# Rows of gate scores spread over the partitions by products in all four batches, in a kernel with an order written out by hand

## The chip, the core and the metric

One core of a Trainium2 chip runs the program. The metric is the device time of one execution in microseconds (us); the median of several runs is compared. Five instruction queues run beside each other: PE (matrix products; its weight loads are shown as PEld), DVE (vector), ACT (scalar), POOL, and SP, which only issues transfers. Each works through its own instructions strictly in order, and waits where an operand or a buffer is not ready. Transfers run on 16 DMA engines.

## What is computed

Four batches of a local attention with block summaries, and behind it a layer in which only the 128 best-scored tokens of a batch go through a two-layer network:

```
scores_l = scale * q @ k.T            # kept where |i - j| < 16
scores_s = scale * q @ max-of-32-keys # plus log(32)
x        = softmax([scores_l, scores_s]) @ [v, mean-of-32-values]
...
scores = einsum('bsd,d->bs', x, w_gate)           # 4 x 768
top    = the 128 largest scores of a batch
out    = x
out[top] = x[top] + sigmoid(scores[top]) * (relu(x[top] @ w1) @ w2)
```

There are 4 batches, 8 heads of 64, 768 tokens, 512 columns, and 1024 hidden columns.

## The kernel before

The heads are taken in pairs (16 pairs, n = 0 to 15, four of each batch), and each pair in three groups of 256 tokens, so that there are 48 steps. The steps of the first three batches go pair by pair; in batch 3 they go group by group over its four pairs. A step i is a chain of short operations: S (scores of two steps at once, PE), M (mask and minimum, DVE), E (exponent, on ACT; on POOL or DVE it is only the subtraction and the exponent comes with the next copy), T (transposes, PE), V (copy out of PSUM, ACT), A (products with the values, PE), R and N (divide, DVE or ACT). Ahead of a pair stand its loads k, q, vt or v, and kmax, vsum, spr, ms, vx, vk, mt, mk, md, which make the block summaries and put the values in place.

Behind the last step of a batch b:

- st{b}.g stores 256 rows of x into the output, ga{b}.u (or gq and gl in batch 3) makes the gate scores of 128 tokens, one column of a 128 x 6 tile `sss` for each u (DVE).
- The 768 scores must then stand as one row in every partition (tile `rows`, 128 x 768). In batches 0 to 2 this is rt (one transpose on PE of the 128 x 6 tile, L412), rk (copy to SBUF on ACT, L415), rw (write of 3 KB to DRAM, L418) and rr (read back, 3 KB into each of the 128 partitions, L421). In batch 3 it is ro and ri: ro{b}.g transposes two score columns, each broadcast to 128 columns (two products on PE, L426), and ri{b}.g copies the 256 columns out of PSUM (ACT or DVE, L430), three times over.
- cmp{b}.u (six of them, L439 and L441, DVE) compares, rank (21 small products), rb, rs, oh, pick and pk make the indices of the 128 tokens, gat (POOL, L504) gathers their rows from the output in DRAM into the tile xe, with fx, fxh, fxl (transpose and split into two parts), f1 (first layer, two halves of three products each), fr, ft, fh, fl (relu, transposes, split), f2 (second layer), fo (scale and add) and sca (POOL, L638), which scatters the rows.
- The weights come in eight loads w0 to w7 through three staging tiles that the network uses again later (h, hh, hl). wh and wl (16 each) split them into a high and a low part, wl always on POOL. So fh0.0, which writes hh, must follow wl13, and fl0.0, which writes hl, must follow wl15.

All order is set by one long text, ORDER, a list of 900 names: `T0@3` is an operation and the PSUM bank it uses, `E4:s` an operation and its engine (v is DVE, s ACT, g POOL). The list is walked once and each name issues its instructions, so each engine's queue is the list's own order, that of SP too. Nothing else moves anything.

Of the kernel before, what the change touches and what calls it, by code (L numbers as in the profile page):

```python
# [54 lines left out]
k0 ones:g zero:v clrv1:g onep0:g q0 onep2:v clrv0:v cst warm@4 kmax0:v spr0:s S0@56 M1.0:v M0.0:v M0.1:v E0:s T0@3 vt0  # L55
M1.1:v vsum0:v casts:v k1 E1:s vt1 onep1:g T1@2 ms0:g vx0.0@5 q1 vk0.0:s vx0.1@1 kmax1:v vk0.1:s spr1:g vx0.2@4 V0:s
vsum1:v V1:v S2@71 vk0.2:s k2 q2 S4@30 k3 M2.1:v M2.0:v M3.1:v A1@5 R1:v ms1:g M3.0:v vt2 N1:s A0@1 E2:g M5.1:v
vx1.2@2 T2@7 R0:v vt3 M4.0:v M4.1:v V2:s vx1.1@4 vk1.1:s vx1.0@5 A2@7 E4:s M5.0:v kmax2:v q3 T4@3 E3:g k4 k5 vt4 w2 q5
q4 vk1.2:s E5:g kmax3:v vk1.0:s R2:v spr2:g T5@6 V4:s S6@02 vsum2:v N0:v vsum3:v M6.1:v M7.0:v spr3:s ms2:s T3@1
M6.0:v V5:s A4@4 R4:v M7.1:v V3:s A5@6 E7:s clrv3:g clrv2:g A3@5 E6:g S8@01 ms3:g N4:v gate R5:v R3:v N2:v vx2.0@4 k6  # L60
N3:s T6@3 vx3.1@2 vsum4:g V6:s M9.0:v N5:v M8.0:v M8.1:v kmax4:v T7@5 vx3.2@3 M9.1:v vk3.1:s vk3.2:v vx3.0@7 vk2.0:s
kmax5:v A6@6 V7:s spr4:s S10@40 E8:s T8@5 w0 V8:s vt6 vx2.2@1 vk3.0:s M10.0:v M11.0:v vx2.1@2 M10.1:v M11.1:v vk2.1:s
vk2.2:s R6:v E10:s E9:g N6:v S12@45 T9@0 M12.0:v A7@3 A8@7 spr5:g wh4:g wl4:g kmax6:v M12.1:v R7:v M13.0:v R8:v E11:g
N7:v V9:s S14@62 E12:s M15.0:v ms4:g wh0:g A9@1 vx4.2@0 M14.1:v T10@3 N8:s R9:v vk4.2:s T12@7 M15.1:v N9:v V10:s
vsum6:g wh5:g M13.1:v vx4.0@0 T11@1 V12:s V11:s q7 ga0.1:v ga0.0:v M14.0:v vt5 vsum5:v ms6:g A10@7 A11@4 R11:v E13:s
vk4.0:s R10:v E14:g spr6:s ms5:s k7 q6 S16@52 N11:v N10:v M16.1:v M17.1:v wl0:g kmax7:v st0.0 vx5.0@4 E15:s ga0.5:v w1
vx4.1@1 k8 T13@6 vk4.1:s T14@2 S18@17 vx5.1@3 M16.0:v V14:s ga0.2:v vk5.0:s A12@2 T15@4 M17.0:v E16:s vk5.1:s vx5.2@0
V15:s vx6.0@3 ga0.3:v M18.1:v V13:s vk6.0:s R12:v E17:g M19.0:v M18.0:v spr7:g wh2:g wh3:g wh1:s wl1:g wl2:g N12:v
vk5.2:s ga0.4:v vx6.2@4 M19.1:v E18:v vx6.1@5 A15@6 vk6.2:s R15:v rt0@0 st0.1 vt7 q8 vsum7:v vk6.1:s rk0:s S20@23
M20.0:v k9 A13@4 M20.1:v R13:v T16@5 N15:s T17@1 A14@0 V16:s A16@6 M21.1:v M21.0:v vt8 ms7:s vx7.0@2 N13:s V17:s  # L70
kmax8:v k10 R14:v R16:v kmax9:v N14:s T18@3 wl3:g V18:s vk7.0:s S22@41 vsum8:v E19:g T19@0 M22.0:v E20:g M22.1:v rw0
M23.1:v T20@7 A18@2 M23.0:v wl5:g E21:g R18:v N16:v spr9:g ms8:s sx0:s spr8:s S24@35 V19:s E23:s vt9 N18:v kmax10:v w4
rr0 A19@4 A17@0 R19:v M24.1:v E22:g M25.1:v R17:v wh8:s vsum9:g k11 q9 T22@2 V22:s vx7.1@1 N19:v N17:v M25.0:v vx8.2@5
vx8.0@4 T21@2 w5 wh9:s q10 vx7.2@0 vk8.2:s vk7.1:s V21:s M24.0:v vx8.1@6 vk8.1:s ms9:s vk7.2:s V20:s cmp0.2:v T23@5
cmp0.5:v vk8.0:v S26@12 sg0:v cmp0.0:v vt10 st0.2 A21@6 wl8:g E24:g sh0:g cmp0.1:v E25:s M27.1:v R21:v M26.1:v M27.0:v
M26.0:v A20@4 vt11 R20:v wh10:s spr10:s T24@3 A22@0 w3 wl9:g N21:s V24:s S28@27 E26:g kmax11:v N20:s V23:s E27:g
vx9.0@1 T25@3 ga1.1:v cmp0.4:v cmp0.3:v M28.0:v vk9.0:s wh11:s vx9.1@4 A23@5 R23:v R22:v A24@6 vk9.1:s V25:s T26@4
rb0:v N23:s V26:s rank0@1 R24:v N22:v vsum11:v S30@35 rs0:v M28.1:v vsum10:g w6 ms10:s vx10.1@4 T27@1 M29.0:v E28:s
wh6:s V27:s M31.0:v M30.0:v T28@0 vk10.1:s M29.1:v vx10.2@2 ga1.2:v vx10.0@7 wl11:g wl10:g N24:v vk10.2:s vk10.0:s
ms11:g st1.0 q11 k13 spr11:s vx9.2@3 vk9.2:s vx11.0@1 vk11.0:s ga1.4:v vx11.2@7 vk11.2:s A25@4 k12 oh0:v ga1.0:v V28:s  # L80
wh12:g pick0@6 fg0:v M31.1:v pk0:v w7 A27@3 S32@21 q12 R27:v vt13 A26@0 ga1.5:v E29:s M30.1:v ga1.3:v gat0:g kmax12:v
N27:s E30:g A28@7 R28:v rt1@3 vx11.1@5 E31:s N28:v rk1:s M33.0:v R26:v T30@6 T29@3 T31@7 vk11.1:s wl6:g V30:s S34@65
V31:s k14 rw1 M32.0:v fx0@2 M32.1:v V29:s E32:s kmax13:v A29@7 M33.1:v R25:v N25:v A30@3 st1.1 M35.0:v M34.1:v fxh0:s
wh13:g T32@4 V32:s N26:s vsum13:v M34.0:v M35.1:v kmax14:v f10.0@1 wh15:g f10.1 A31@0 sx1:s sg1:v R29:v fxl0:v vt12
rr1 vsum12:v q13 E33:s vt14 v12.0 A32@4 E35:s R31:v N31:v R32:v spr12:g wl12:g wl15:g wh7:g f10.3@6 wl7:g cmp1.0:v
vt15 st1.2 f10.2 N29:s T33@2 k15 q14 mt12@5 fr0.0:s wh14:g f10.4 V33:s N32:s R30:v E34:g wl13:g wl14:g f10.5 N30:v
cmp1.2:v vsum14:g mt13@1 T34@0 cmp1.5:v mk12:s md12.1 v13.0 ft0.0@4 T35@2 fr0.1:s spr13:s V34:s fh0.0:s V35:s ft0.1@5
md12.0 cmp1.3:v vsum15:g sh1:g cmp1.1:v S36@76 fl0.0:v M37.0:v A35@2 A34@0 A33@3 cmp1.4:v M37.1:v mk13:s M36.1:v R35:v
fh0.1:s E37:s rb1:v N35:s f20.0@1 M36.0:v rank1@4 f20.1 rs1:v R33:v N33:s oh1:v ga2.0:v md13.1 E36:s kmax15:v R34:v
N34:s spr15:g T37@4 f20.2 pick1@2 mt14@6 mk14:s spr14:s f20.3 f20.4 T36@0 fl0.1:v pk1:v ga2.5:v V37:s V36:s ga2.3:v  # L90
fg1:v ga2.2:v q15 S38@73 v12.1 M38.1:v S40@05 ga2.1:v mt15@6 md13.0 mk15:s md14.0 gat1:g M39.1:v v13.1 f20.5 ga2.4:v
fo0.0:v fx1@2 fxh1:s A36@4 v15.1 M38.0:v sx2:s fxl1:v M40.0:v R36:v M39.0:v rt2@6 M40.1:v sca0:g rk2:s f11.3@1 E38:g
E39:v f11.4 S42@37 N36:s M41.1:v A37@4 M41.0:v R37:v T38@6 E41:g M42.0:v v15.0 E40:s M43.1:v M42.1:v f11.5 T39@2 E42:g
T40@7 N37:s V39:s S44@40 M43.0:v sg2:v E43:g S46@23 M44.1:v M45.1:v v14.0 md14.1 M44.0:v rw2 M45.0:v V38:s v14.1 V40:s
T41@5 A38@0 E44:g sh2:g V41:s A40@7 M46.1:v M47.0:v M47.1:v T43@4 rr2 md15.0 T44@6 A41@5 md15.1 A39@3 R38:v N38:v
M46.0:v cmp2.0:v V43:s T42@4 E45:g st2.0 R40:v N40:v cmp2.5:v R39:v E47:s st2.1 cmp2.1:v cmp2.3:v E46:s f11.0@2 R41:v
N41:v fr1.1:s V42:s gq3.1:v cmp2.4:v gq3.0:v T46@0 f11.1 f11.2 A43@4 N39:s R43:v A42@3 R42:v V44:s fr1.0:s cmp2.2:v
ft1.0@6 fh1.0:s ft1.1@1 T47@5 T45@7 N43:s V46:s N42:v rb2:v rank2@3 A44@2 fl1.0:v gl3.0:v V45:s A46@0 V47:s gl3.1:v
A45@6 A47@5 rs2:v fh1.1:s oh2:v R46:v R47:v pick2@4 st2.2 fg2:v pk2:v fl1.1:v R45:v ro3.0@7 gq3.2:v R44:v ri3.0:v
N47:s N46:s N45:s gq3.3:v f21.0@3 f21.1 f21.2 gat2:g f21.3 N44:s gl3.2:v cmp3.1:v gl3.3:v gq3.4:v cmp3.0:v ro3.1@1  # L100
fx2@6 f21.4 f21.5 fxh2:s gq3.5:v ri3.1:v gl3.4:v cmp3.2:v gl3.5:v f12.3@2 ro3.2@4 f12.0@5 f12.1 cmp3.3:v ri3.2:s sx3:s
fxl2:v f12.2 fo1.0:v f12.4 sca1:g cmp3.4:v cmp3.5:v rank3@7 rb3:v sg3:v f12.5 sh3:g st3.2 st3.0 fr2.0:s ft2.0@5 rs3:v
oh3:v pick3@1 fg3:v pk3:v fr2.1:s ft2.1@0 fh2.0:s fh2.1:s fl2.0:v f22.0@7 f22.1 f22.2 f22.3 st3.1 gat3:g fl2.1:v fx3@6
f22.4 f22.5 fxh3:v f13.0@5 fo2.0:v sca2:g f13.1 fxl3:v f13.2 f13.3@7 f13.4 f13.5 fr3.0:v ft3.0@4 fr3.1:v ft3.1@0
fh3.1:v fh3.0:s fl3.0:v f23.0@3 f23.1 f23.3@6 f23.4 f23.5 f23.2 f23.6 fl3.1:v f23.9 f23.7 f23.8 fo3.0:v f23.10 f23.11
fo3.1:v sca3:g
# [4 lines left out]
def attn_moe(ctx: ExitStack, tc: tile.TileContext, q, k, v, vt, vs, w1, w2, cst, line, out, cap):  # L111
# [50 lines left out]
    srow = [const.tile([NU, 128], F32, name=f"srow{i}") for i in range(1)]  # L162
# [20 lines left out]
    def put(name, engs, fn, *a):  # L183
        ops[name] = (engs, fn, a)
# [224 lines left out]

    def rows_turn(e, b):  # L410
        rps[b] = ps = bank("m")
        nc.tensor.transpose(out=ps[0:NU, 0:128], in_=s_(b), identity=ident)  # L412

    def rows_keep(e, b):
        copiers[e](out=srow[0], in_=rps[b][0:NU, 0:128])  # L415

    def rows_write(e, b):
        nc.sync.dma_start(out=line[b].rearrange("(u t) -> u t", u=NU), in_=srow[0])  # L418

    def rows_read(e, b):  # L420
        nc.sync.dma_start(out=rank_tiles(b)[0], in_=line[b].unsqueeze(0).broadcast_to([128, S]))  # L421

# [317 lines left out]
    for b in range(B):  # L740
        for g in range(NG):
# [10 lines left out]
            if b == B - 1:  # L752
                put(f"ro{b}.{g}", "t", rows_of, b, g)
                put(f"ri{b}.{g}", "sv", rows_into, b, g)
        if b < B - 1:
            put(f"rt{b}", "t", rows_turn, b)
            put(f"rk{b}", "sv", rows_keep, b)
            put(f"rw{b}", "d", rows_write, b)
            put(f"rr{b}", "d", rows_read, b)
# [106 lines left out]
```

## Time and profile before

| | us |
|---|---|
| median of 3 runs | 171.59 (171.19 to 171.59) |
| the profiled execution | 172.67 |
| its span, first to last instruction | 170.4 |
| busy in the span: PE / DVE / ACT / POOL | 157.7 / 137.7 / 107.8 / 88.2 |
| granted TensorE clock | 1.00 |

Busy time of an engine is the time in which at least one of its instructions runs; matrix products are pipelined, so the step from one group's start to the next group's start (its pitch) is often shorter than the duration of one. Views speak of the span, whose zero is the first instruction. The profiled execution lies 2.3 us above its span and 1.1 us above the median.

### The profile page before, as it was taken

How to read it: one execution, taken by the hardware profiler on the slowest of the kernel's cores; microseconds unless marked ns; L12 is line 12 of the kernel's file. 1: busy time of each engine (PE TensorE's matmuls, PEld its weight loads, DVE VectorE, ACT ScalarE, POOL GpSimd, SP SyncE). 2: the span in 40 equal slices, each digit the busy share in tenths (PEclk: the TensorE clock that was granted, in tenths of full speed). 3: DMA queues.
4: the chain of work that ended last, by engine and by line, in shares of the span. 5: the costliest groups of instructions: out<-in, count | busy, mean ns of one | idle time of the engine just before them, and what ended most of it. 6: DMA issues, size and time to landing. Idle time of an engine off the chain costs nothing.

```text
span 170.4 us, 6154 instructions
## 1 busy us (share of the span) xinstructions
PE 157.7 (93%) x2273; PEld 128.9 (76%) x2273; DVE 137.7 (81%) x718; ACT 107.8 (63%) x319; POOL 88.2 (52%) x134
## 2 busy tenths in 40 slices
PE   7979999998999979899899999699999999999980
PEld 2448788887878968788787978478889787788870
DVE  4297999999999989999999799686899997533620
ACT  0365888998989799899978785264778721300100
POOL 7013787985499968965999823406510204202002
PEclk9999999999999999999999999999999999999999
DMA  5999999989998999999888995978600292101001
GB/s 204 349 414 419 410 381 367 319 310 314 347 335 321 260 368 383 369 361 348 298 311 258 317 205 94 270 202 278 222 1 4 63 349 86 50 12 62 4 0 62
DMA packets 14897, 41.44 MB, mean 243 GB/s; under 512 B 1538, under 2 KB 2708, under 8 KB 14868
## 3 DMA queue, kind: packets, MB, share of 16 engines
q1 hardware_dynamic: 14228, 38.95, 66.1%
q0 software_dynamic: 640, 2.10, 3.8%
q8 instruction: 18, 0.29, 0.7%
q14 instruction: 11, 0.09, 0.1%
HBM read 33.10 MB, written 7.35 MB: 237 GB/s over the span
## 4 chain that ended last, share of the span: by engine, by line
PE 38%; DVE 20%; issue 14%; DMA 12%; POOL 7%; ACT 5%; POOLq 1%; SPq 0%; DVEq 0%
PE z_A_a L354 8%; PE z_T_t L337 7%; PE z_S_sa L305 6%; DVE sm L317 4%; PE z_warm_m L673 4%; DVE lt L439 4%; DMA rows<-line 4%; PE z_f10p_f L571 3%; DMA xe<-out_dram,idx 3%; DMA line<-srow 3%; DVE lt L441 3%; ACT p L328 2%; DMA hl<-in_w_dram 2%; POOL p L331 2%; PE z_S_sb L305 2%
## 5 line engine op out<-in xcount | busy, mean ns | idle before, releaser
L328 ACT ACTIVATE p<-sm,mxs 128x120 f32<-128x120 f32 x92 | 29.1, 399 | 5.0 <-DVE mxs L317 4.9
L331 POOL TENSOR_TENSOR p<-sm,mxs 128x480 f32<-128x480 f32 x23 | 23.5, 1026 | 15.6 <-PE z_T_t L337 6.1
L337 PE MATMUL z_T_t<-cs,p 128*120 128x128 f32 x192 | 29.5, 280 | 1.5 <-ACT p L328 1.2
L354 PE MATMUL z_A_a<-v,pt 121*64 121x65 f32 x768 | 29.1, 225 | 0.1
L354 PEld LDWEIGHTS z_A_a<-v,pt 121*64 121x64 f32 x768 | 24.9, 137 | 5.2 <-issue 1.8
L305 PE MATMUL z_S_sa<-slots,qb 64*64 64x120 f32 x384 | 25.6, 269 | 0.9 <-DMA qb<-in_q_dram 0.9
L337 PEld LDWEIGHTS z_T_t<-cs,p 128*120 128x120 f32 x192 | 21.5, 137 | 6.0 <-ACT p L328 2.8
L305 PE MATMUL z_S_sb<-slots,qb 64*64 64x120 f32 x384 | 24.9, 268 | 1.2 <-issue 0.6
L317 DVE CUSTOM_DVE_ANT_0 sm<-z_S_sa,cs 128x120 f32<-128x120 f32 x96 | 22.3, 275 | 4.4 <-PE z_S_sb L305 3.5
L370 ACT ACTIVATE x<-z_A_a,rdens 128x64 f32<-128x64 f32 x96 | 22.0, 329 | 5.1 <-DVE rdens L359 5.0
L317 DVE CUSTOM_DVE_ANT_0 sm<-z_S_sb,cs 128x120 f32<-128x120 f32 x96 | 22.3, 275 | 2.8 <-PE z_S_sb L305 2.6
L305 PEld LDWEIGHTS z_S_sa<-slots,qb 64*64 64x64 f32 x384 | 19.9, 132 | 5.1 <-issue 2.9
L305 PEld LDWEIGHTS z_S_sb<-slots,qb 64*64 64x64 f32 x384 | 19.6, 132 | 0.9 <-ACT x L370 0.8
L638 POOL DMA_INDIRECT out_dram<-h,idx x4 | 4.0, 996 | 28.7 <-DVE h L632 28.7
L344 ACT ACTIVATE pt<-z_T_t 120x512 f32<-120x512 f32 x25 | 15.2, 611 | 5.8 <-PE z_T_t L337 3.8
L229 DVE TENSOR_REDUCE kss<-slots 128x24 f32<-128x768 f32 x16 | 15.0, 943 | 1.3 <-DMA slots<-in_k_dram 1.3
L317 DVE DVE_READ_ACCUMULATOR2_ANT mxs<- 128x1 f32 x192 | 15.8, 82 | 0.0
L342 ACT COPY pt<-z_T_t 120x512 f32<-120x512 f32 x22 | 12.9, 600 | 3.3 <-PE z_T_t L337 3.0
L399 DVE SCALAR_TENSOR_TENSOR junkv<-x,cs 128x512 bf16<-128x512 f32 x18 | 13.0, 724 | 0.1
L439 DVE TENSOR_SCALAR_CACHE_REDUCE lt<-rows,sss 128x256 bf16<-128x256 f32 (+4 forms) x20 | 12.0, 601 | 0.5 <-DMA rows<-line 0.5
L504 POOL DMA_INDIRECT xe<-out_dram,idx x4 | 4.7, 1184 | 14.5 <-DVE idx L499 11.5
L373 DVE TENSOR_TENSOR x<-z_A_a,rdens 128x256 f32<-128x256 f32 x24 | 9.7, 414 | 0.3
(195 smaller groups left out, 329.8 us busy)
## 6 DMA issues: line engine op xcount, KB each, us to landing
slots<-in_k_dram SPq DMA_DIRECT2D x16, 552.0 KB
slots<-in_vs_dram SPq DMA_DIRECT2D x12, 552.0 KB
qb<-in_q_dram SPq DMA_DIRECT2D x16, 384.0 KB
out_dram<-x SPq DMA_DIRECT2D x12, 512.0 KB
v<-in_v_dram SPq DMA_DIRECT2D x8, 292.5 KB
hl<-in_w_dram SPq DMA_DIRECT2D x3, 512.0 KB
hh<-in_w_dram SPq DMA_DIRECT2D x3, 512.0 KB
slots<-in_vt_dram SPq DMA_DIRECT2D x4, 384.0 KB
```

The source lines that it names most:

```text
L229: nc.vector.tensor_reduce(out=ks.rearrange("p (u m) -> p u m", u=NU), in_=kv, axis=AX.X, op=ALU.max)
L305: nc.tensor.matmul(out=sc[k][h][par * QT:(par + 1) * QT, uu * NC:(uu + 1) * NC], lhsT=qt[rows, t * QT:(t + 1) * QT], rhs=kt[rows, window(t ...
L317: nc.vector.tensor_tensor_reduce(out=sm[:, j, :], in0=sc[i][h][:, uu * NC:(uu + 1) * NC], in1=cs[:, c0:c0 + NC], scale=-1.0 / D ** 0.5, sc ...
L328: nc.scalar.activation(out=pb[i % 3][:, j, :], in_=sm[:, j, :], func=AF.Exp, scale=-1.0, bias=mx[:, j:j + 1])
L331: engines[e].tensor_tensor(out=pb[i % 3], in0=sm, in1=mx.unsqueeze(2).broadcast_to([128, 4, NC]), op=ALU.subtract)
L337: nc.tensor.transpose(out=ps[0:NC, j * 128:(j + 1) * 128], in_=pb[i % 3][:, j, :], identity=ident)
L342: copiers[e](out=dst, in_=src)
L344: nc.scalar.activation(out=dst, in_=src, func=AF.Exp, scale=-1.0)
L354: nc.tensor.matmul(out=av[par * QT:(par + 1) * QT, j, :], lhsT=pt[0:NC + 1, j, par * QT:(par + 1) * QT], rhs=vw[n % NVB][0:NC + 1, par, u, ...
L370: nc.scalar.activation(out=x_(b, g)[:, j // 2, c:c + D], in_=av[:, j, 0:D], func=AF.Copy, scale=rden[:, j:j + 1])
L399: nc.vector.scalar_tensor_tensor(out=junkv, in0=x_(b, u // 2)[:, u % 2, :], scalar=1.0, in1=gate, op0=ALU.mult, op1=ALU.mult, accum_out=s_ ...
L439: nc.vector.tensor_scalar(out=lt[u][:, 0:c], in0=rows[:, 0:c], scalar1=s, scalar2=0.0, op0=ALU.is_lt, op1=ALU.add, accum_out=accs[:, b % 2 ...
```

## The change

The rows are made by ro and ri in all four batches. rt, rk, rw and rr go, with the tile `srow` and the DRAM lines. And the list is a new one from its first name to its last: it holds 906 names instead of 900, and nearly every operation stands at another place; some are on another engine (exponents: 23 on POOL, 23 on ACT, 2 on DVE before; 26, 21, 1 now. vsum: 6 on POOL before, 5 now. N: 24 on ACT before, 22 now. wh: 10 on POOL before, 8 now). Of the new ri, eleven are on ACT and one on DVE.

```
 ORDER = """
-k0 ones:g zero:v clrv1:g onep0:g q0 onep2:v clrv0:v cst warm@4 kmax0:v spr0:s S0@56 M1.0:v M0.0:v M0.1:v E0:s T0@3 vt0
...
-fxl2:v f12.2 fo1.0:v f12.4 sca1:g cmp3.4:v cmp3.5:v rank3@7 rb3:v sg3:v f12.5 sh3:g st3.2 st3.0 fr2.0:s ft2.0@5 rs3:v
...
+k0 onep1:v clrv2:v cst vt0 zero:v warm@1 casts:v kmax0:v clrv3:g q0 onep2:v spr0:g k1 onep0:g S0@17 q1 clrv0:g vsum0:v
...
+ri3.2:s cmp3.5:v cmp3.2:v cmp3.4:v f12.4 sg3:v rank3@4 rb3:v rs3:v sca1:g fr2.0:s st3.1 ft2.0@0 f12.5 sh3:g fh2.0:s
...
-    def rows_turn(e, b):
-        rps[b] = ps = bank("m")
-        nc.tensor.transpose(out=ps[0:NU, 0:128], in_=s_(b), identity=ident)
-
-    def rows_keep(e, b):
-        copiers[e](out=srow[0], in_=rps[b][0:NU, 0:128])
-
-    def rows_write(e, b):
-        nc.sync.dma_start(out=line[b].rearrange("(u t) -> u t", u=NU), in_=srow[0])
-
-    def rows_read(e, b):
-        nc.sync.dma_start(out=rank_tiles(b)[0], in_=line[b].unsqueeze(0).broadcast_to([128, S]))
...
-            if b == B - 1:
-                put(f"ro{b}.{g}", "t", rows_of, b, g)
-                put(f"ri{b}.{g}", "sv", rows_into, b, g)
-        if b < B - 1:
-            put(f"rt{b}", "t", rows_turn, b)
-            put(f"rk{b}", "sv", rows_keep, b)
-            put(f"rw{b}", "d", rows_write, b)
-            put(f"rr{b}", "d", rows_read, b)
+            put(f"ro{b}.{g}", "t", rows_of, b, g)
+            put(f"ri{b}.{g}", "sv", rows_into, b, g)
```

Three places of the new order. First, the start of DVE's queue, up to its first work on keys (zero feeds the 16 warming products on PE; pt and v are buffers that are cleared). Before:

```order
L667 MEMSET zero 128x1
L664 MEMSET pt_78 32x512
L654 MEMSET v_72 32x24x64
L655 MEMSET v_72 32x24
L656 MEMSET v_72 120x24
L229 TENSOR_REDUCE kss<-slots 128x24
```

And now:

```order
L650 MEMSET pt_77 32x512
L640 MEMSET v_74 32x24x64
L641 MEMSET v_74 32x24
L642 MEMSET v_74 120x24
L653 MEMSET zero 128x1
L669 CAST iotab<-cs 128x128
L670 TENSOR_SCALAR tri<-cs 128x128
L671 CAST tok<-cs 128x24x2
L228 TENSOR_REDUCE kss<-slots 128x24
```

The memset of zero now stands behind one pt and one v buffer, and the three casts that need the constants stand ahead of the first kmax.

Second, SP's queue around the write and the read back of batch 0 (slots are the loads of keys and values, qb those of queries, hh and hl weights on their way). Before:

```order
L418 DMA line<-srow_105 6x128
L217 DMA slots<-in_vs_dram 128x1104
L517 DMA hh<-in_w_dram 128x1024
L421 DMA rows<-line 128x768
L206 DMA slots<-in_k_dram 128x1104
L210 DMA qb_68<-in_q_dram 128x768
L517 DMA hl<-in_w_dram 128x1024
L210 DMA qb_69<-in_q_dram 128x768
```

And now:

```order
L378 DMA out_dram<-x_87 128x2x512
L503 DMA hh<-in_w_dram 128x1024
L216 DMA slots<-in_vs_dram 128x1104
L503 DMA hl<-in_w_dram 128x1024
L205 DMA slots<-in_k_dram 128x1104 x2
L209 DMA qb_69<-in_q_dram 128x768
```

The two transfers of the score row are gone; the load into qb_69 still follows the weights of hl.

Third, PE's queue from the last product of rank1 to the first of pick1 (oh is what pick multiplies). Before:

```order
L450 MATMUL z_rank_m<-one,lt_115 128x1
L624 MATMUL z_f20p_y<-w2l,hh 128x512 x4
L337 MATMUL z_T_t<-cs,p_93 120x128 x4
L624 MATMUL z_f20p_y<-w2h,hl 128x512 x4
L493 LDWEIGHTS oh
```

And now:

```order
L436 MATMUL z_rank_m<-one,lt_114 128x1
L577 MATMUL z_ft0p_f<-cs,h 128x128 x4
L610 MATMUL z_f20p_y<-w2h,hh 128x512 x4
L610 MATMUL z_f20p_y<-w2l,hh 128x512 x4
L610 MATMUL z_f20p_y<-w2h,hl 128x512 x4
L610 MATMUL z_f20p_y<-w2h,hh 128x512 x4
L479 LDWEIGHTS oh
```

Between rank1 and pick1 stood two groups of f2 and one T; now there are four groups of f2 and one half's ft.

## Rows read from the trace of the kernel before

**Rows 1.** The page, part 1: busy us, share, instructions of each engine.

```profile
PE 157.7 (93%) x2273; PEld 128.9 (76%) x2273; DVE 137.7 (81%) x718; ACT 107.8 (63%) x319; POOL 88.2 (52%) x134
```

**Rows 2.** Busy time by window: start:end, length, each engine, clock, DMA share, GB/s.

```profile
21.00:99.00 78.00, 74.72 (x1356) 63.95 (x1355) 74.67 (x410) 69.16 (x203) 64.54 (x93) 1.00 0.95 330
81.00:91.00 10.00, 9.40 (x131) 7.79 (x132) 9.76 (x50) 8.61 (x29) 9.92 (x12) 1.00 0.86 289
110.00:165.00 55.00, 54.45 (x588) 45.92 (x588) 38.54 (x197) 22.62 (x69) 11.62 (x18) 1.00 0.32 107
```

**Rows 3.** Timeline of PE: start, duration, line, [idle before <- releaser]: turn and ro.

```profile
48.21 0.27 PE L412 MATMUL z_rt_m<-cs,sss 128*6 128x128 f32 x1 [0.27 <-ACT v L284]
48.42 0.31 PE L305 MATMUL z_S_sa<-slots,qb 64*64 64x120 f32 x1
...
139.63 0.38 PE L426 MATMUL z_ro3p_m<-cs,sss 128*128 128x128 f32 x2
139.77 1.18 PE L571 MATMUL z_f12p_f<-w1h,xh 128*128 128x512 f32 x4
```

**Rows 4.** Lines L426, L415 and L430: count, duration ns min/median/max, first and last start.

```profile
L426 PE MATMUL z_ro3p_m<-cs,sss x6: 271/272/302, 132.1 to 139.7; 128*128 128x128 f32 x6
L415 ACT COPY srow<-z_rt_m x3: 238/248/255, 49.0 to 110.9; 6x128 f32<-6x128 f32 x3
L430 ACT COPY rows<-z_ro3p_m x1: 374/374/374, 140.0 to 140.0; 128x256 f32<-128x256 f32 x1
```

**Rows 5.** Chain that ended last, in time: start, us, what; then one row of waits.

```profile
54.35 6.24 DMA rows<-line
```

```profile
DVE lt L439 <- DMA rows<-line: 0.5, 1, 0.5
```

**Rows 6.** Timeline of SP, then of PE: a query load and the scores behind it.

```profile
58.16 0.66 SPq L210 DMA_DIRECT2D qb<-in_q_dram  x1
```

```profile
62.97 0.31 PE L305 MATMUL z_S_sa<-slots,qb 64*64 64x120 f32 x1 [0.86 <-DMA qb<-in_q_dram]
```

**Rows 7.** Timeline of PE: rank1, pick1, and the transposes behind the gather of batch 1.

```profile
99.19 0.68 PE L450 MATMUL z_rank_m<-one,lt 128*128 128x1 bf16 x21
102.11 0.30 PE L493 MATMUL z_pick_m<-tok,oh 128*128 128x5 bf16 x6
```

```profile
109.38 0.63 PE L544 MATMUL z_fx_m<-cs,xe 128*128 128x128 f32 x4 [1.60 <-DMA xe<-out_dram,idx]
```

**Rows 8.** Timeline of all engines at the start, down to the scores S6.

```profile
0.92 6.53 PE L673 MATMUL z_warm_m<-zero 128*128 128x512 bf16 x16 [0.92 <-DVE zero L667]
1.02 0.48 DVE L664 MEMSET pt<- 32x512 f32 x1 [0.16 <-issue]
...
1.78 1.34 DVE L654 MEMSET v<- 32x1536 f32 x1 [0.27 <-issue]
...
9.66 2.45 PE L337 MATMUL z_T_t<-cs,p 128*120 128x128 f32 x8 [1.23 <-ACT p L328]
...
20.97 0.31 PE L305 MATMUL z_S_sa<-slots,qb 64*64 64x120 f32 x1
```

**Rows 9.** Timeline of all engines near the end.

```profile
140.81 1.00 POOL L638 DMA_INDIRECT out_dram<-h,idx  x1 [6.91 <-DVE h L632]
...
144.05 0.60 ACT L580 ACTIVATE h<-z_f12p_f 128x512 f32<-128x512 f32 x1 [3.52 <-DMA out_dram<-h,idx]
```

```profile
158.18 0.60 PE L591 MATMUL z_ft3p_f<-cs,h 128*128 128x128 f32 x4
159.13 0.66 PE L591 MATMUL z_ft3p_f<-cs,h 128*128 128x128 f32 x4 [0.35 <-DVE h L582]
159.54 0.72 PE L624 MATMUL z_f23p_y<-w2h,hh 128*128 128x256 f32 x4
```

**Rows 10.** A row of waits, then a group of instructions: busy us, mean ns, idle before.

```profile
DVE hl L536 <- POOL vss L246: 1.1, 1, 1.1
```

```profile
L529 POOL TENSOR_TENSOR w2l<-hl,w2h 128x512 fp32r<-128x512 f32 x4 | 5.1, 1293 | 0.0
```

## What the change was predicted to do

> **What bounds the kernel now.** I read the busy times first, then the windows, then the waits and the chain, and last the timeline at the few places where PE stops. PE is busy for 157.7 of 170.4 us [rows 1], and the windows show how: from 110 to 165 us it is busy 54.45 of 55 us [rows 2], so in that last third the end is simply the sum of PE's work, whatever the other engines do. From 21 to 99 us PE and DVE are both busy 74.7 of 78 us and ACT 69.2 [rows 2]; there three engines hand short pieces to each other, and a loss on any of them is soon one of PE. The clock is granted in full in every window. The time is therefore PE's work plus the few places where PE stops. What the change takes away, in batch 0 a read back of 6.24 us behind its write, stands on the chain that ended last, but the only wait for it in the whole trace is 0.5 us of DVE [rows 5]: the transport itself was covered. So the removal pays where it held up other things, and the products have to be paid on the busiest engine.
>
> **The products.** Batches 0 to 2 get nine ro of two products each and lose three rt. By pitch, a pair of products moved PE's next start by 0.14 us and the rt by 0.21, which was late itself by 0.27 us [rows 3]; I take 0.20 for a pair, a little over its row, since in the middle more of them will come between unlike work, and 0.15 for an rt: 9 x 0.20 - 3 x 0.15 = **+1.35 us**. Bounds: by full duration, 272 ns for each product [rows 4], it would be 18 x 0.272 - 3 x 0.273 = +4.1 us; nothing at all if every pair falls into a stop of PE. I choose the pitch because in the middle PE has a next instruction ready nearly always.
>
> The Trainium skill, "TensorE: Matmul & The Clock Gate", Part 4: PE-mode transpose, gives about 275 ns for a 128 x 128 transpose inside a kernel, most of it access latency. The 272 ns rows agree with the figure, but the pitch says that the latency overlaps with the next instruction; by the page's figure as a cost the products would be an estimated +4.1 us instead of +1.35.
>
> **The copies and the other engines.** Nine ri at 0.374 us less three rk at 0.248 us [rows 4] are +2.6 us on ACT. The new list takes two exponents and two N off ACT and gives three exponents to POOL, which loses a vsum and two wh in turn. No engine's total moves by more than about its own slack of the middle stretch, so I put this at 0, with a bound of 1.0 us either way for the stretch where ACT and DVE are nearly full.
>
> **SP's queue.** Before, the read back waits for its write to land; behind it, in the order shown above, stand a weight load and a query load that starts only at 58.16 us, and PE stops 0.86 us for exactly such a query load at 62.97 [rows 6]. In the new queue nothing waits for a score row, and the weight load ahead of the query load finds its staging tile free earlier, because the list consumes that tile (wl5) some forty names sooner. I take the stop away whole: **-0.86 us**. Cover for this: if another load comes late in its place, the term is 0.
>
> **The gather of batch 1.** From rank1 to the transposes fx1 there are 109.38 - 99.19 = 10.2 us, and at the end PE stops 1.60 us for the gathered rows [rows 7]. PE reaches pick1 2.9 us after rank1 starts [rows 7]; in the new queue two more groups of f2 (1.18 us for a like group of four from first start to last end [rows 3], less where they follow each other) and one ft stand there in the place of a T, about 2 us. Pick1 then comes later than the one-hot rows need, the gather starts perhaps a microsecond later, and PE has 2 us more to do meanwhile: the stop shrinks by about a microsecond, **-1.0 us** (bounds -1.6 and 0). The work itself is not saved, only moved under the gather.
>
> **The start.** The memset of zero now follows a pt memset of 0.48 us and a v memset of 1.34 us [rows 8] with their gaps and two small ones, so the warming products, 6.53 us of them, start near 3.2 instead of 0.92 us, and the first scores come 2.3 us later. Bounds: +2.3 us if nothing takes that up, and -0.4. In the trace of before, PE then waits 1.23 us for the first exponents and spreads eight transposes over 2.45 us [rows 8]; the new list does vsum0, kmax0 and the casts ahead of the scores and runs twelve vx transposes and two further S while the first exponents are made on POOL. PE reaches the scores S6 at 20.97 us [rows 8], 13.5 us after the end of the warming products (0.92 + 6.53 = 7.45). In these lie the 1.23 us and what the eight transposes spend beyond their pitch, 2.45 - 8 x 0.07 = 1.9 us [rows 3, 8]: 3.1 us of waiting, more than the 2.3 us that are lost. I take **0**.
>
> **The end.** Two changes. The second half of the transposes ft3 stopped 0.35 us for its relu [rows 9]; now products of f2 stand between the halves: **-0.35 us**. Against that, ft2.0 now stands directly behind rank3 and ahead of f12.5. Its relu fr2.0 must wait until the scatter of batch 1 has left the tile h; before, that took from 140.81 to 144.05 us, 3.24 us [rows 9], and f12.5 covered it. Now three compares, rank3 and nothing else cover it, which leaves PE standing between 0 and 1.0 us; I take **+0.3 us**, under the middle, since PE may itself be late at rank3.
>
> The sum: 1.35 - 0.86 - 1.0 + 0 - 0.35 + 0.3 = -0.56 us. It is made against the profiled execution: its span goes from 170.4 to 169.8, and its 172.67 us to 172.1, since the 2.3 us around the span are not touched. That execution lay 1.1 us above the median of the runs, so the median goes from 171.59 to **171.0 us**. A measurement of this kernel tells a difference from none at about 0.3%, that is 0.5 us; the forecast lies just on the faster side of it. With the gather's stop gone whole, no loss at ft2.0 and a further microsecond from the middle stretch it would be 171.0 - 0.6 - 0.3 - 1.0, about 169.0.
>
> **The rivals.** *Hidden anyway (same, 171.6):* the transport was covered, only 0.5 us was ever waited for [rows 5], and the stops of 0.86 and 1.6 us just turn up at other names of a new list that asks the same engines for the same work. Then the products' 1.35 us stand against the gains at the end and half of the two stops, about 0. For it: PE and DVE are equally full in the middle, so no single cure frees PE there. Against it: two of the stops have a named cause that is gone or better covered.
>
> *Weights late at the first network (slower, 173.0):* the list puts the loads w6 and w7 60 and 80 names later, with the network of batch 0 at the same place. POOL splits them, 1.29 us for each wl [rows 10], and is busy 9.92 of 10 us there already [rows 2]. At the end of that queue now stand sh1, wh13, wl13, wl15, and fh0.0 and fl0.0 must wait for wl13 and wl15, since they overwrite the staging tiles; DVE's fl0.0 waited 1.1 us for POOL before [rows 10]. If POOL ends wl13 later than PE ends ft0.1, each further microsecond stops PE ahead of f20.0. With a lag of one wl and one wh, about 2 us, the time is 171.0 + 2 = 173.0. Against it: POOL no longer has two vsum in that place, and its work ahead is spread more evenly.
>
> *The start is not taken up (slower, 173.4):* 171.0 + 2.3, rounded up. It decides whether PE reaches S6 at 21 or at 23 us.
>
> *The products cost their duration (slower, 173.8):* 171.0 + 4.1 - 1.35, if a broadcast score column can't be streamed behind other products as the two ro rows were. The page named above gives the same for its figure taken as a cost.
>
> **How the numbers follow.** Forecast, faster than 171.1: 0.42. Hidden anyway, within 0.3%: 0.22. Weights late 0.20, start 0.11, products 0.05, together 0.36 slower by over 0.3%. The range reaches down to 169.0, the forecast with its terms at their good ends, and up to 173.3, which takes in the late weights and most of a lost start.
>
> **What would show it.** Of the changed kernel: no row rows<-line; the pitch of a pair of ro on PE at 0.14 to 0.30 us; the scores S6 starting near 21 us although the warming products end near 9.7; no stop of PE for a query load; fx1 with less than 0.8 us of idle time ahead; ft3 in two halves without a stop; a stop of at most 1 us ahead of ft2.0. It would be wrong if PE is idle for fh0.0 or f20 with POOL's wl as the releaser, if S6 starts at 23 us, or if the stretch from S6 to rank1, 78.2 us before, grows by more than 1.5 us because DVE or ACT now falls behind at other places.

## The result, and the profile after

The changed kernel takes **173.14 us** (median of 20 runs, 171.96 to 174.81) beside 171.59 us for the kernel before: ratio 1.0082, 95% interval 1.0056 to 1.0108. A second measurement of the same kernel (e1 below) gave 173.25 us and 1.0088 [1.0048, 1.0128]. So the change makes the kernel slower by about 1.5 us (0.8%), where 171.0 us, slightly faster, had been forecast. Some executions of a kernel are slower than the rest (over 1.5% above its fastest): medians take them in, ratios leave them out, and since the profiled execution of the first measurement was one of them, all rows of "after" below are those of e1, 173.30 us with a span of 171.5.

The busy times and the windows, which answer to [rows 1, 2]. First the page's part 1 of the changed kernel:

```profile
PE 156.3 (91%) x2288; PEld 129.4 (75%) x2288; DVE 139.1 (81%) x720; ACT 107.8 (63%) x312; POOL 87.6 (51%) x129
```

Then its busy time by window (columns as in [rows 2]):

```profile
21.00:99.00 78.00, 74.73 (x1367) 64.31 (x1364) 74.44 (x405) 67.63 (x198) 61.50 (x88) 1.00 0.94 321
81.00:91.00 10.00, 10.00 (x173) 8.66 (x165) 9.93 (x52) 9.02 (x30) 9.60 (x13) 1.00 0.98 339
110.00:165.00 55.00, 52.81 (x581) 44.24 (x576) 39.73 (x191) 23.91 (x68) 10.52 (x17) 1.00 0.31 103
```

PE has 1.4 us less of busy time in all, and the kernel is slower: PE now stands idle. From 110 to 165 us it was busy 54.45 of 55 us before and is busy 52.81 now. The loss has to be looked for there.

Next the steps that the prediction wanted to see, from the timeline of PE in the changed kernel (start, duration, line, [idle before <- releaser]):

```profile
3.27 6.33 PE L659 MATMUL z_warm_m<-zero 128*128 128x512 bf16 x16 [3.27 <-DVE zero L653]
...
21.37 0.31 PE L304 MATMUL z_S_sa<-slots,qb 64*64 64x120 f32 x1
...
97.49 0.68 PE L436 MATMUL z_rank_m<-one,lt 128*128 128x1 bf16 x21
...
108.55 0.38 PE L412 MATMUL z_ro2p_m<-cs,sss 128*128 128x128 f32 x2
108.77 0.60 PE L530 MATMUL z_fx_m<-cs,xe 128*128 128x128 f32 x4
...
127.31 0.65 PE L577 MATMUL z_ft1p_f<-cs,h 128*128 128x128 f32 x4 [0.93 <-DVE x L372]
```

The warming products start at 3.27 us and S6 still starts near 21 us; a pair of ro moves PE's next start by 0.22 us; fx1 has no stop ahead of it, where 1.60 us stood [rows 7]. Up to here the forecast is met.

Now the end. The timeline of all engines in the changed kernel, cut to the second scatter from last, the relu of batch 3 and the last scatter:

```profile
153.62 1.00 POOL L624 DMA_INDIRECT out_dram<-h,idx  x1 [5.08 <-DVE gsb L546]
...
157.61 0.60 ACT L566 ACTIVATE h<-z_f13p_f 128x512 f32<-128x512 f32 x1 [5.30 <-DMA out_dram<-h,idx]
...
158.26 0.66 PE L577 MATMUL z_ft3p_f<-cs,h 128*128 128x128 f32 x4 [0.99 <-ACT h L566]
...
166.10 0.48 DVE L618 SCALAR_TENSOR_TENSOR h<-z_f23p_y,gsb,xe 128x256 f32<-128x256 f32 x1 [0.94 <-PE z_f23p_y L610]
167.37 0.98 POOL L624 DMA_INDIRECT out_dram<-h,idx  x1 [12.76 <-issue]
```

The same places in the kernel before (beside the ft3 rows of [rows 9]):

```profile
153.81 0.99 POOL L638 DMA_INDIRECT out_dram<-h,idx  x1 [6.31 <-DVE h L632]
...
156.67 0.69 DVE L582 TENSOR_SCALAR h<-z_f13p_f 128x512 f32<-128x512 f32 x1 [2.54 <-DMA out_dram<-h,idx]
...
165.52 0.48 DVE L632 SCALAR_TENSOR_TENSOR h<-z_f23p_y,gsb,xe 128x256 f32<-128x256 f32 x1 [0.47 <-PE z_f23p_y L624]
166.28 0.98 POOL L638 DMA_INDIRECT out_dram<-h,idx  x1 [11.48 <-DVE h L632]
```

Two things are late. The relu of batch 3 overwrites the tile h and so waits until the scatter of batch 2 has read it. The products that its first half reads end at 154.32 + 1.09 = 155.41 us now and ended at 155.54 us before; it starts 2.2 us later now and started 1.1 us later before. From the scatter's issue to the relu it is 157.61 - 153.62 = 3.99 us now and was 156.67 - 153.81 = 2.86 us; PE stops 0.99 us for it. And the last scatter is issued 167.37 - (166.10 + 0.48) = 0.79 us after DVE's last instruction, where it was 0.28 us.

Taken apart at the first product of f13 and at the end of PE's last product (both from the timeline of PE), with four kernels from below:

| us | before | after (e1) | e2 | e6 | e11 | e9 |
|---|---|---|---|---|---|---|
| f13.0 starts | 152.58 | 152.39 | 152.23 | 152.69 | 152.36 | 151.64 |
| from there to PE's last end | 12.90 | 13.67 | 12.40 | 12.53 | 12.60 | 12.40 |
| from there to the span's end | 4.95 | 5.46 | 5.45 | 5.46 | 4.94 | 4.94 |

The loss of e1 is in the second and third line: 0.77 + 0.51 = 1.28 us.

Why the scatter is late stands in the view of the DMA queues. It shows, over a stretch cut in 40 slices, the GB/s moved, then the packets, MB and share of 16 engines of each queue, and from issue to landing in us. The kernel before, 153 to 158 us:

```profile
GB/s 0 0 0 0 0 0 0 0 0 0 0 0 0 0 0 0 0 0 33 426 393 426 295 426 99 0 0 0 0 0 0 0 0 0 0 0 0 0 0 0
...
q0 software_dynamic: 80, 0.26, 13.8%
issues: line engine op xcount, KB each, median us to landing
out_dram<-h,idx POOLq DMA_INDIRECT x1, 2.7
```

The changed kernel, 153 to 158 us:

```profile
GB/s 0 0 0 0 0 0 0 0 0 0 0 0 0 0 0 0 131 295 360 295 426 360 230 0 0 33 0 33 0 33 33 0 0 0 0 0 0 0 0 0
...
q0 software_dynamic: 80, 0.26, 14.0%
q8 instruction: 1, 0.02, 1.4%
issues: line engine op xcount, KB each, median us to landing
out_dram<-h,idx POOLq DMA_INDIRECT x1, 3.9
```

In the changed kernel a packet of kind "instruction" runs in the same stretch: 16 KB (0.02 MB), 1.4% of 16 x 5 us = 1.1 us on one DMA engine. The bulk of the scatter takes seven slices (0.9 us) in both, but in the changed kernel four more slices of 33 GB/s (one packet of 4 KB each in 0.125 us) trail behind it, and the landing comes after 3.9 us, not 2.7. By the packet records of the trace the instruction packet runs from 155.08 to 156.20 us, and the four that trail start at 156.20 us, when it ends. In the kernel before, the last such packet starts at 158.5 us, when that scatter has landed.

The change itself brings the packet there. PE's products up to the start of f13.0, before and now (window: busy PE, count, clock, DMA share, GB/s):

```profile
0.00:152.57 152.57, 145.18 (x2193) 1.00 0.78 268
0.00:152.38 152.38, 143.66 (x2208) 1.00 0.75 261
```

Fifteen products more (18 of ro less 3 of rt) stand ahead of f13.0, each with a weight load, so 30 entries of PE's program. The last packet starts 2.7 us after f13.0 now (155.08 - 152.39) and started 5.9 us after it before. The experiments e5 to e7 move it.

### The profile page after: what moved, and what is told of

Read it like the earlier page. It is cut to its first block, busy times and chain, and to the rows that moved or that the text cites. A ratio compares the mean times of both kernels' runs of the same rounds, so it can differ in the third digit from the quotient of the medians.

```text
span 173.0 us, 6165 instructions
## 1 busy us (share of the span) xinstructions
PE 156.2 (90%) x2288; PEld 130.5 (75%) x2288; DVE 139.0 (80%) x720; ACT 107.8 (62%) x312; POOL 87.8 (51%) x129
## 5 line engine op out<-in xcount | busy, mean ns | idle before, releaser
L330 POOL TENSOR_TENSOR p<-sm,mxs 128x480 f32<-128x480 f32 x26 | 27.2, 1053 | 20.6 <-PE z_T_t L336 12.6
L353 PE MATMUL z_A_a<-v,pt 121*64 121x65 f32 x768 | 27.8, 224 | 0.6 <-ACT pt L343 0.6
L336 PE MATMUL z_T_t<-cs,p 128*120 128x128 f32 x192 | 27.8, 277 | 0.5 <-POOL p L330 0.5
L327 ACT ACTIVATE p<-sm,mxs 128x120 f32<-128x120 f32 x84 | 27.0, 412 | 1.1 <-PE z_A_a L353 0.6
L304 PE MATMUL z_S_sa<-slots,qb 64*64 64x120 f32 x384 | 24.6, 268 | 1.5 <-POOL v L642 1.0
L369 ACT ACTIVATE x<-z_A_a,rdens 128x64 f32<-128x64 f32 x88 | 20.0, 334 | 1.5 <-DVE rdens L358 1.5
L341 ACT COPY pt<-z_T_t 120x512 f32<-120x512 f32 x20 | 12.0, 604 | 3.2 <-PE z_T_t L336 2.5
L398 DVE SCALAR_TENSOR_TENSOR junkv<-x,cs 128x512 bf16<-128x512 f32 x18 | 13.6, 753 | 0.0
L425 DVE TENSOR_SCALAR_CACHE_REDUCE lt<-rows,sss 128x128 bf16<-128x128 f32 (+4 forms) x20 | 11.9, 597 | 0.3 <-ACT rows L416 0.3
L239 DVE TENSOR_REDUCE vss<-slots 128x24 f32<-128x768 f32 x11 | 10.3, 939 | 0.9 <-DMA slots<-in_vs_dram 0.9
```

The lines of the kernel that those rows point to most:

```text
L304: nc.tensor.matmul(out=sc[k][h][par * QT:(par + 1) * QT, uu * NC:(uu + 1) * NC], lhsT=qt[rows, t * QT:(t + 1) * QT], rhs=kt[rows, window(t ...
L327: nc.scalar.activation(out=pb[i % 3][:, j, :], in_=sm[:, j, :], func=AF.Exp, scale=-1.0, bias=mx[:, j:j + 1])
L330: engines[e].tensor_tensor(out=pb[i % 3], in0=sm, in1=mx.unsqueeze(2).broadcast_to([128, 4, NC]), op=ALU.subtract)
L336: nc.tensor.transpose(out=ps[0:NC, j * 128:(j + 1) * 128], in_=pb[i % 3][:, j, :], identity=ident)
L341: copiers[e](out=dst, in_=src)
L353: nc.tensor.matmul(out=av[par * QT:(par + 1) * QT, j, :], lhsT=pt[0:NC + 1, j, par * QT:(par + 1) * QT], rhs=vw[n % NVB][0:NC + 1, par, u, ...
```

## Experiments

Each ratio is against runs of the kernel before made beside the experiment on the same chip: 171.70 us for e1 to e4, 172.00 for e5 to e8, 171.53 for e9 to e12, which ran on another chip.

### e1: the changed kernel once more

No edit.

> The changed kernel as it is, for a second profile on the chip of the runs beside it. Theory A (the tile h, still held by the scatter of batch 2, stops PE ahead of ft3.0, and the clock falls behind the stop): PE idle 1 to 2 us ahead of ft3.0, the clock below 1.00 in the 5 us behind it, f13.0 reached about 1 us earlier than before; 1.006 to 1.011 of before. Theory B (the products and the new middle cost it): f13.0 reached later than the 152.58 us of before.

173.25 us, 1.0088 [1.0048, 1.0128]. The loss is there again, and its rows stand above. Of theory A the stop is there, at 0.99 us, but not the rest: f13.0 starts only 0.19 us earlier than before, and the granted clock is 1.00 behind the stop too (160 to 165 us).

### e2 and e4: another home for the relu of batch 3

```
-        ff["h"] = hs
+        ff["h"] = hs if b < B - 1 else slots_[:, 0:FF]
```

e2 has it in the changed kernel, so that this relu need not wait for the scatter of batch 2; e4 has it in the kernel before.

> The changed kernel, but batch 3's relu writes into columns of the tile of keys, which nothing reads any more by then, instead of into h, so that it waits for no scatter; one line. Theory A: no stop of over 0.4 us ahead of ft3.0, the clock at 1.00 to the end, 1.5 to 3 us less than the changed kernel: 170.2 to 171.7, so at or under before. Theory B: within 0.5 us of the changed kernel, about 173.

> The kernel before with the same one line as e2: batch 3's relu into the tile of keys. Theory A: before loses its stops ahead of ft3 too, which its trace shows at 0.35 us but which vary with the scatter; 0.3 to 1.0 us less than before, 170.6 to 171.3. Theory B has no reason for a gain: 171.6 within 0.3.

e2: 171.33 us, 0.9982 [0.9948, 1.0015], that is 1.9 us less than e1. e4: 171.54 us, 1.0037 [0.9994, 1.008], nothing gained, where 0.3 to 1.0 us had been expected. The timeline of e2:

```profile
155.29 0.60 ACT L566 ACTIVATE slots<-z_f13p_f 128x512 f32<-128x512 f32 x1 [3.15 <-PE z_f13p_f L557]
...
156.95 0.60 PE L577 MATMUL z_ft3p_f<-cs,slots 128*128 128x128 f32 x4
```

The relu follows PE and no longer the scatter, and there is no stop ahead of ft3. The scatter itself is as late as ever in e2 (4.6 us to its landing, with an instruction packet beside it); nobody waits for it. So this wait makes up the larger part of the loss; in the kernel before, f13.4 and f13.5 ahead of the transposes cover it as long as no packet falls on the scatter (e7 below shows it with one).

### e3: cover for the wait

```
-f13.4 fr3.0:s ft3.0@5 fh3.0:s f13.5 fl3.0:v
+f13.4 f13.5 fr3.0:s ft3.0@5 fh3.0:s fl3.0:v
```

> The changed kernel with one name moved: f13.5 ahead of fr3.0 and ft3.0, as the list of before had it, so that one more group of products (0.93 us) covers the scatter. Theory A: the stop ahead of ft3.0 is shorter by 0.9 us, 0.8 to 1.5 us less than the changed kernel, 171.6 to 172.3. Theory B: no gain, or 0.3 us more for the second half's relu.

173.25 us, 1.0085 [1.0046, 1.0124]: no gain, as theory B had it. The timeline of PE in e3 shows both stops:

```profile
157.89 0.66 PE L577 MATMUL z_ft3p_f<-cs,h 128*128 128x128 f32 x4 [0.94 <-ACT h L566]
159.28 1.22 PE L610 MATMUL z_f23p_y<-w2h,hh 128*128 128x256 f32 x8 [0.73 <-ACT hh L591]
```

In this execution f13.0 starts at 151.13 us and the scatter at 152.37, and the relu comes only at 157.24, 4.9 us later. One product group of 0.93 us does not cover that, and what it filled, the making of hh behind the transposes, is bare now.

### e5, e6 and e7: moving the instruction packet

```
-WARM = 16
+WARM = 32        # e5, e7 (e7: in the kernel before); 2 in e6
```

There are 18 instruction packets of 16 KB in a trace, all on queue q8, and PE issues 2288 products and as many weight loads: one packet for about 256 entries of its program. The Trainium skill ("Runtime: NRT & Kernel Launch", Instruction fetch mechanics) says the same, blocks of 16 KiB or 256 instructions that the sequencer fetches itself over a DMA queue, and calls the cost "mostly hidden"; no wait of PE here names its program, but the runs below show what a packet does to a transfer beside it. More or fewer products of zeros at the start leave all later work as it is, and shift the points at which the packets come.

> The changed kernel with 32 products of zeros at the start in place of 16: 32 more entries in TensorE's program (a weight load and a matmul each), in a stretch where TensorE only waits for the first loads. Theory fetch (the scatter of batch 2 is late because a 16 KB instruction packet, TensorE's program read ahead, takes one of the DMA engines at 154.2 to 156.0 us, where four of the scatter's packets wait behind it): the packets come about one per 256 entries, so this one comes some 3 us earlier and is over before the scatter; scatter's start to the relu of batch 3 falls from 5.0 and 4.0 us to 2.9 +- 0.3, the stop ahead of the first turn of batch 3 from 0.99 us to under 0.3, and the time to 172.2 us (171.8 to 172.7). Rival, what the scatter writes or POOL's work makes it late: the scatter still takes 4 us or more and the time stays at 173.2 (172.9 to 173.6). If the products of zeros cost time at the start the time would rise by at most 0.9 us, and the start of the sixth pair's scores would show it.

> The changed kernel with 2 products of zeros at the start in place of 16: 28 entries fewer ahead of all that follows. Theory fetch: the instruction packet of 154.2 us comes 3 us later, at some 157.3, after the scatter; scatter's start to relu 2.9 +- 0.3 us, stop ahead of the first turn of batch 3 under 0.3 us, time 172.2 us (171.8 to 172.7). Rival, something else makes the scatter late: 4 us or more, and 173.2 us. If fewer products leave the clock low at the start, that shows as a lower granted clock up to 20 us, and adds some tenths to either.

> The kernel before with 32 products of zeros in place of 16. Theory fetch: its last instruction packet moves from 158.5 us, after the scatter, to about 154.8, into it; the scatter's start to relu rises from 2.9 to 4 us or more, the stop ahead of the first turn of batch 3 from 0.35 to 1.0 to 1.6 us, and the time to 172.6 us (172.1 to 173.0). Rival, something else makes the scatter of the changed kernel late: scatter to relu stays at 2.9 and the time at 171.6 (171.3 to 172.0).

e6: **171.72 us**, 0.9989 [0.9956, 1.0023], 1.5 us less than the changed kernel and just under the range expected. Its queues from 153 to 158 us, and then from 157 to 161 us:

```profile
q0 software_dynamic: 80, 0.26, 13.8%
issues: line engine op xcount, KB each, median us to landing
out_dram<-h,idx POOLq DMA_INDIRECT x1, 2.7
```

```profile
q8 instruction: 1, 0.02, 1.5%
```

And its timeline, where the relu now starts 2.84 us after the scatter's issue (153.93 us) and PE passes without a stop:

```profile
156.77 0.60 ACT L566 ACTIVATE h<-z_f13p_f 128x512 f32<-128x512 f32 x1 [4.17 <-DMA out_dram<-h,idx]
...
157.42 0.66 PE L577 MATMUL z_ft3p_f<-cs,h 128*128 128x128 f32 x4
```

e7 is the reverse, a hit in the kernel before. Its queues, 155 to 160 us, then its timeline (the scatter is issued at 155.66 us):

```profile
GB/s 0 0 0 0 0 0 0 0 0 0 0 0 0 0 0 0 0 360 229 459 295 459 262 33 0 0 0 0 0 0 0 33 0 0 33 0 33 33 0 0
...
q8 instruction: 1, 0.02, 2.1%
issues: line engine op xcount, KB each, median us to landing
out_dram<-h,idx POOLq DMA_INDIRECT x1, 4.7
```

```profile
160.49 1.29 DVE L582 TENSOR_SCALAR h<-z_f13p_f 128x512 f32<-128x512 f32 x2 [4.51 <-DMA out_dram<-h,idx]
...
161.23 1.25 PE L591 MATMUL z_ft3p_f<-cs,h 128*128 128x128 f32 x8 [1.04 <-DVE h L582]
```

Scatter to relu 4.83 us instead of 2.86, a stop of 1.04 us instead of 0.35, as the theory wanted. In e7 the packet ends at 158.90 us, and the four packets that trail start at 158.89. In e5 the packet starts at 157.7 us, before the scatter of 159.25; that lands after 2.7 us, the relu follows 2.85 us after its issue, and PE passes. In all three the packet moved against f13.0 by about 3 us, in the direction forecast. In e7 the cover of f13.4 and f13.5 is in place, and the stop is there all the same: it is the packet and not the lost cover that decides.

The times of e5 and e7 miss their expectations by far: 177.0 us (1.0205 [1.0147, 1.0263], which is 175.5 us of 172.0) and 177.59 us (1.034 [1.0299, 1.038]). I had taken 16 products of zeros for 0.9 us; that was the wait ahead of them, their duration is 6.3 us. The first scores S0 start at 13.22 us in e5 against 9.71, and at 10.27 in e7 against 7.38, and none of it is taken up: the scores S6 start at 24.89 us in e5 against 21.37, and at 23.85 in e7 against 20.97. By the ratios e5 lies 2.0 us above e1; the late start of 3.5 us, less the 1.1 us by which the way from f13.0 to the span's end is shorter (18.03 against 19.12 us), would be 2.4. In e7 the start is 2.9 us, and with the 1.2 us of PE's longer way from f13.0 to its end (14.09 against 12.90 us) 4.1 of 5.6 us; the rest stays open. For the cause these two count by their rows around the scatter, not by their times. e6 has no such confusion: S0 comes 1 us earlier there, and f13.0 0.3 us later.

### e9 and e11: the last scatter's two waits

```
-f13.4 fr3.0:s ft3.0@5
+f13.4 fr3.0:v ft3.0@5
```

e9 is e2 with this, e11 is e6 with this. The last scatter reads columns 0 to 511 of h. fr3.0 writes all of them, and fo3.0 and fo3.1 on DVE then write one half of them each. In the changed list fr3.0 is on ACT, in the one before on DVE.

> The second kernel (the changed one with the relu of batch 3 into the first key tile) with the first half of that relu on VectorE in place of ScalarE, so that one engine writes all that the last scatter reads. Theory wait (the last scatter is issued 0.79 us after VectorE's last instruction in the changed kernel against 0.28 before, since GpSimd waits there for VectorE and ScalarE one after the other): the last scatter is issued 0.3 us after VectorE's last instruction, and the time falls from 171.33 to 170.8 us (170.5 to 171.1). Rival, the 0.5 us lies in the scatter itself or in TensorE's last products: the distance stays at 0.8 us and the time at 171.3 (171.0 to 171.7).

> The changed kernel with 2 products of zeros at the start (as in e6) and the first half of the relu of batch 3 on VectorE: both causes of the loss taken away, without the second home for the relu. If the instruction packet on the scatter (1.0 us) and GpSimd's second wait (0.5 us) are the whole of what the forecast missed, 171.2 us (170.8 to 171.6), 2 us under the changed kernel. Rival, the wait of GpSimd is nothing: 171.7 as e6.

e9: **170.70 us**, 0.9944 [0.9911, 0.9977], faster than both kernels. e11: 171.22 us, 0.9985 [0.9951, 1.0019]. From e2 to e9 the ratio falls by 0.4%, about 0.6 us; from e6 to e11 it falls by no more than 0.1 us, well inside the intervals, so that there the gain is shown by the rows and not by the time. The end of e9:

```profile
164.08 0.48 DVE L618 SCALAR_TENSOR_TENSOR slots<-z_f23p_y,gsb,xe 128x256 f32<-128x256 f32 x1 [0.94 <-PE z_f23p_y L610]
...
164.85 0.98 POOL L624 DMA_INDIRECT out_dram<-slots,idx  x1 [10.98 <-DVE slots L618]
```

The scatter is issued 0.29 us after DVE's last instruction, and from PE's last end to the span's end it is 4.94 us, in e11 too. The waits of POOL in the changed kernel and in e9 (waited for: us, times, longest) name the difference; with fr3.0 on ACT the view names no releaser and says "issue":

```profile
POOL out_dram L624 <- issue: 12.8, 1, 12.8
```

```profile
POOL out_dram L624 <- DVE slots L618: 11.0, 1, 11.0
```

That one relu on ACT costs 0.5 us, 9 us after it has ended. The rival, time lost in the scatter itself, falls. That POOL waits for DVE and ACT one after the other is the likely reason, but no view shows the second wait. In batch 2 the relu is on ACT too, and its scatter is issued 0.28 us after DVE's last instruction (153.62 against 152.59 + 0.75 us in e1); there fo2.0 writes all 512 columns at once. So it isn't ACT as such, but fits an early write on another engine that no single later write covers.

### e10: the price of a pair of products

```
-        for u in (2 * g, 2 * g + 1):
+        for u in (2 * g, 2 * g + 1) * (1 if b == B - 1 else 2):
```

> The kernel of e9 with each pair of spreading products of batches 0 to 2 issued twice, 9 pairs more of the kind whose price was in dispute. Theory pitch (a pair takes 0.15 to 0.3 us of TensorE's time): +1.8 us over e9 (+1.2 to +2.5). Rival, a pair costs its recorded duration of 0.54 us: +4.9 us. Rival, TensorE has slack around them: less than +0.7.

172.46 us, 1.0032 [0.9994, 1.0069]: 1.76 us more than e9 by the medians, 1.5 by the ratios, for 9 pairs, so 0.17 to 0.20 us each. One pair in e9 and the same pair issued twice in e10, timelines of PE:

```profile
107.71 0.38 PE L412 MATMUL z_ro2p_m<-cs,sss 128*128 128x128 f32 x2
107.93 0.60 PE L530 MATMUL z_fx_m<-cs,xe 128*128 128x128 f32 x4
```

```profile
109.31 0.60 PE L412 MATMUL z_ro2p_m<-cs,sss 128*128 128x128 f32 x4
109.75 0.60 PE L530 MATMUL z_fx_m<-cs,xe 128*128 128x128 f32 x4
```

0.22 us for two products, 0.44 for four. The price by pitch stands, and the price by duration (4.9 us) falls.

### e8 and e12: the products with the list of before

```
-k9 A13@4 M20.1:v R13:v T16@5 N15:s T17@1
+k9 A13@4 ro0.1@7 ri0.1:s M20.1:v R13:v T16@5 N15:s T17@1 ro0.2@7 ri0.2:s
...
-N28:s rk1:s M33.0:v
+N28:s ri1.0:s M33.0:v
```

The list of before with ro and ri in the places of rt and rk and a few names on, in batches 0 to 2, and no rw or rr.

> The changed kernel's products and copies for all four batches, but with the list of before: the three turns of batches 0 to 2 stand where the one turn stood and within some 10 entries behind it, the writes to DRAM and reads back are gone, all else as before. Theory products (a pair of them costs 0.15 to 0.3 us of TensorE's time, 9 pairs for 3 turns of 0.21): +0.7 to +2.0 us ahead of the end, less the 0.86 us wait for a query load that the SP queue no longer causes; time 172.0 us (171.2 to 172.9). Rival, a pair costs its recorded duration of 0.54 us: +4.2 less 0.9, 174.9 us. Rival, the removed transport is worth more than the products: under 171.2. TensorE's program grows by the products' entries, so the last instruction packet moves too; where it falls on the scatter of batch 2, 1 us is to be added to either.

> The kernel of e8 once more, for its interval and a profile that nothing disturbs: +1.9 us over the kernel before in e8. Theory products: a turn's place at 0.27 to 0.36 us a pair, 9 pairs less 3 turns of 0.2 us, gives +2.1, less the wait for a query load; 173.2 us (172.4 to 174.0). Rival, the larger part is the gathers of batches 0 and 1 coming later (stops of 1.3 and 2.1 us ahead of them in e8 against 0.6 and 1.6): then these stops are there again and the products account for 1 us or less.

e8: 174.45 us, 1.0113 [1.0056, 1.017]. e12: 176.63 us, 1.0257 [1.0197, 1.0317]. The same program thus lay 1.9 and 4.4 us above the kernel before by the ratios (2.5 and 5.1 by the medians), more than the 172.0 and 173.2 us expected, and the two measurements don't agree. By its median e8 lies near the 174.9 us of the price by duration; e10 is what speaks against that price. As the expectation allowed for, a packet falls on the scatter of batch 2 in both traces: 2208 products stand ahead of f13.0, and the packet starts 2.6 and 2.7 us after it. From f13.0 to the span's end it is 18.16 us in e8 and 18.93 in e12 against 17.85, so 0.3 and 1.1 us are lost there, with 3.96 and 4.71 us from scatter to relu. In e12's trace PE also stops 1.46 us ahead of fx0, where it stopped 0.57 before, and the window around it has a granted clock of 0.83, as has that from 10 to 20 us (window: busy PE, clock, DMA share, GB/s):

```profile
85.96 1.03 PE L530 MATMUL z_fx_m<-cs,xe 128*128 128x128 f32 x4 [1.46 <-DMA xe<-out_dram,idx]
```

```profile
80.00:90.00 10.00, 8.11 (x103) 0.83 0.84 293
```

So with the old list the products gain nothing: the stops ahead of the gathered rows stay (1.46 and 0.64 us in e12, 0.57 and 1.60 before). How much of the rest is products, how much the stops and how much a lower clock can't be told from these two.

## Why the prediction was wrong, point by point

- **The products** (+1.35 us): right as a price on PE. A pair's pitch is 0.14 to 0.31 us in e1 and its price 0.17 to 0.20 us in e10, where 0.20 was taken. Their recorded duration is 272 ns as before and is no price here. The Trainium skill ("TensorE: Matmul & The Clock Gate", Part 4: PE-mode transpose) gives about 275 ns for a 128 x 128 transpose inside a kernel; the row agrees as a duration, and e10 decides against it as a cost. What the prediction did not have is their second price: their 30 entries move the instruction packet onto the scatter.
- **SP's queue** (-0.86 us) **and the gather of batch 1** (-1.0 us): the mechanisms are right. In the changed kernel no stop of PE has a query load as its releaser, and the 1.60 us ahead of fx1 are gone whole. But other stops came: 0.93 us ahead of ft1.1, and 0.8 us ahead of an S for ACT.
- **The start** (0): right within 0.4 us. S6 starts at 21.37 us against 20.97, though the warming products end 2.2 us later. In e6, with S0 1 us earlier, S6 is no earlier (21.44 us). But that used the slack up: e5's further 3.5 us come through whole.
- **The sum up to f13.0** was 1.35 - 0.86 - 1.0 + 0.3 = -0.21 us, and profile against profile it is -0.19. This agreement should not be leaned on. The profiled execution of before lay 1.1 us above its median, and since the list of before needs 17.85 us from f13.0 to the span's end in its profiled execution and 17.86 in e4's, all of that lay ahead of f13.0. An estimate by the medians (median less the time around the span less f13.0 to the end, against the kernel before measured beside it) puts f13.0 later than before by 0.0 to 0.5 us in e2, e6, e9 and e11, and by 0.7 us in e1; so these terms together were 0.2 to 0.9 us too good, and which of them stays open. And the 2.3 us around the span, which were to stay, are 1.8 us in all kernels with the new list: 0.5 us gained that nobody forecast. By this estimate the 1.5 us of e1 are 0.7 ahead of f13.0 and 1.28 behind it, less 0.5 around the span.
- **The end** (-0.35 us for ft3): this is the step that failed; it came out at **+1.28 us**. The stop of 0.35 us between the halves of ft3 did go. But the prediction looked at PE's neighbours alone. The reading that from 110 to 165 us the end is PE's work "whatever the other engines do" fell with it. That the relu of batch 3 already waited for the scatter of batch 2 (DVE idle for 2.54 us, the last 1.1 us of them behind the products it reads) stood in the trace of before, covered by f13.4 and f13.5; the new list moved f13.5 behind the transposes and so took half of the cover away, and that wait was put at nothing. The similar wait of batch 2, which was priced, came to nothing: no stop ahead of ft2.0. Without a hit 2.84 us from issue to relu just pass (e6), even with the lost cover; with one there is a loss even with the full cover (e7, e12). The packet that hits adds 1.1 us or more to the relu's wait. The second loss, 0.5 us at the last scatter, comes from one letter of the list, fr3.0 on ACT instead of DVE.
- **The forecast without these two** is e11, which takes both away and nothing else but 14 products of zeros: 171.22 us beside a forecast of 171.0. That it comes so near is in part luck. By the ratio e11 is 0.3 us under the kernel before (no clear difference), where 0.6 was forecast, and 0.5 us of it come from the time around the span; span against span it is about 0.15 us longer by the medians (169.44 against 169.29 us), not 0.56 us shorter.
- **The rivals**: that the weights come late, that the start isn't taken up and that the products cost their duration all fell. The result lies where they would have put it, for another reason. *Hidden anyway* missed by its time, 171.6 us, but its picture fits the stretch up to f13.0, where stops came back at other names.

How far each cause is settled: that the relu's wait for the scatter is the larger loss is shown (e2), and that the instruction packet makes the scatter late is shown both ways (e6 by time and rows, e5 and e7 by rows). The trace does not name the DMA engine of a packet; that the two share one is read from the four packets that start when it ends. The size of a hit varies with how long the packet takes and where in the scatter it falls: scatter to relu was 4.0 us in e1 (a packet of 1.1 us), 4.9 in e3 and 4.8 in e7 (1.7 us each). That fr3.0 on ACT delays the last scatter is shown by rows in two pairs (e2 and e9, e6 and e11); the second wait of POOL is argued.

## What to carry to other kernels

Before taking the cover off a wait, price the wait whole, a buffer's release by a transfer above all: its usual length in the trace, and what it would be if one of its last packets came a microsecond late. Count the instructions that a change adds ahead of such a wait, since they move the packets of the program too. In this kernel a tile of its own for the last stage (e2) was worth more than a finer order around the shared one (e3). When an early write to a tile changes its engine, look at the transfer that reads the tile at the very end: here that cost 0.5 us although the write had ended 9 us before.

## What the runs showed of the hardware that was not expected

- TensorE's own program comes in by 16 KB packets beside the data. There are 18 of them in an execution, and each takes 0.9 to 2.7 us. When one runs during a scatter of 80 packets, four of those start only when it ends, and the scatter lands after 3.8 to 4.8 us instead of 2.7 (e1, e2, e3, e7, e8, e9, e12). Adding or taking away 28 to 32 entries of the program, at its start (e5, e6, e7) or in batches 0 to 2 (e8, e12), moves the packet by 3 us, so that a change to one stage can alter another stage that it does not touch.
- A transfer instruction on POOL whose tile was written by ACT and then, half by half, by DVE was issued 0.79 us after DVE's last instruction, against 0.28 us when DVE had written all of it.
- With 2 products of zeros instead of 16, and 4.44 us of idle time behind them, the first scores take 0.40 us each and not 0.26 (e6), while the granted clock of that window stands at 1.00, the level of 2.4 GHz. What makes them slower is not shown.
